# Packed attention with a gated feed-forward: the first product of six of eight batches as Strassen's seven block products

## The chip, the core and the metric

The kernel runs on one core of a Trainium2 chip. A core has four compute engines: TensorE (PE in the profile; its weight loads have a row of their own, PEld), VectorE (DVE), ScalarE (ACT) and GpSimd (POOL). SyncE (SP) issues the transfers here. Each engine takes its instructions in the order in which they are written, and engines wait for each other by semaphores. TensorE writes only to PSUM, which has eight banks of 512 float32 columns. The metric is the device time of one execution in microseconds, as a median of runs.

## The reference

Inputs: q, k, v of 8 batches x 8 heads x 576 rows x 64, p of 8 x 8 x 32 x 64, w_a and w_b of 512 x 1536, w_out of 1536 x 512.

```python
def sm_attn(qq, kk, vv):
    s = scale * np.matmul(qq, kk.transpose(0, 1, 3, 2))
    s = s - np.max(s, axis=-1, keepdims=True)
    a = np.exp(s)
    a = a / (np.sum(a, axis=-1, keepdims=True) + 1e-09)
    return np.matmul(a, vv)
p_packed = sm_attn(p, k, v)             # 32 packed rows per head
out = sm_attn(q, p_packed, p_packed)    # 576 rows attend to the 32 packed rows
...
x = out, heads side by side             # 4608 tokens x 512
a = x @ w_a
b = x @ w_b
return (a * b @ w_out)
```

## The kernel before

All of it is float32. Since `out` of a head is a2 (the second softmax, 576 x 32 per head) times the head's 32 packed rows, `x @ w_a` is a2 times a matrix G that has 256 rows (8 heads x 32) and is made for each batch from the packed rows and the weights. The **first product** of a batch is thus a2 (576 tokens x 256) times G (256 x 1536, for w_a and for w_b), the **second** is the gated h (576 x 1536) times w_out. In both, each operand is split in a high part of reduced precision (fp32r) and a rest, and high x high, high x rest and rest x high are added up in PSUM: three matmuls for each block product.

A batch runs through 12 feature tiles `ft` of 128 features. `mm1` (L378) makes one: `mm1_half` (L365) twice, for w_a and w_b, each 2 blocks of the 256 rows x 3 terms x 2 halves of the tokens = 12 matmuls of 128 x 288, so 24 per tile. ACT copies the w_a half (L385), DVE multiplies (L388), ACT takes the high part of h (L392), POOL the rest (L86 `h_lo`). `mm2_part` (L396) is the second product: 36 matmuls of 128 x 512 for a tile of 128 tokens; four or five token tiles per batch (a batch has 4.5, and odd batches do the shared one). It runs after all 12 feature tiles.

G is made by `g_tiles` (L341, matmuls at L355) from the weights in `w_ab`, which stay in SBUF, and split by ACT (L361) and DVE (L86 `glo`). These matmuls use TensorE as eight small tiles of 64 rows x 32 columns, one for each pair of a head group and a half; so do the attention products (L249 and L309 in 64 x 32, L293 in 128 x 32). The other matmuls and the transposes use the whole 128 x 128 array. Per batch `g_tiles` is called at three feature tiles (`G_AT`) and once for the next batch.

The attention of batch b+1 is cut into steps, and a table (`PLAN`) puts them between the halves of the feature tiles and between the parts of the second product of batch b; the order of each engine is as the code writes it. Batch 0 also converts the weights; it has tables of its own. PSUM: two pairs of banks (`m`) for the products, one pair (`s`) for the attention, two single banks (`x`) for G.

Of the kernel before, what the change touches and what calls it, by code (L numbers as in the profile page):

```python
# [19 lines left out]
def tile_packed_attn_gated_ffn(  # L20
# [25 lines left out]
    P = 128  # L46
# [8 lines left out]
    NT = 5  # L55
    scale = 1.0 / float(D) ** 0.5
# [3 lines left out]
    big = ep(tc.tile_pool(name="big", bufs=1))  # L60
    ld = ep(tc.tile_pool(name="ld", bufs=1))
# [8 lines left out]
    scratch = early.__enter__()  # L70

# [4 lines left out]
    w_ab = big.tile([P, NC, R, 4 * P], F32, name="w_ab")  # L76
# [154 lines left out]
    def turned(dst, src, back=0):  # L231

        tp = bank()
# [5 lines left out]
    pp = {}  # L239
# [62 lines left out]
    def stage2(b, e):  # L302

        TU = 2 * XH
        hi, lo = (t[:, e, :].rearrange("p (x u l) -> p u x l", u=2, l=TL) for t in (a2_hi, a2_lo))
        x = bank_pair(b == 1 or e == 0)
# [22 lines left out]
        a2f = work(b, f"a2f_{e}", [P, 2, XH, TL], "t2")  # L329
        nc.vector.transpose(out=a2f.rearrange("p u x l -> p (u x l)"), in_=s2.rearrange("p x j -> p (x j)"))  # L330
        nc.scalar.copy(out=hi, in_=a2f)
# [6 lines left out]
    ghi = ld.tile([P, E, 4, 2 * P], F32R, name="ghi")  # L338
    glo = ld.tile([P, E, 4, 2 * P], F32R, name="glo")
# [102 lines left out]
    def emit(b, plan, tasks={}):  # L442

        for name in plan.split():
# [45 lines left out]
    PLAN = (" |  |  | S0 | r0 | r0 |  | r0 |  | r0 Lv1 ; S1 | r1 | q0 Lk2 | r1 | r1 |  | r1 q1 Lk3 Lv2 |  |  |  | "  # L490
            "| T2 P0 |  |  | s0 s0 s1 g s0 |  | s1 | Lp4 s0 s1 s1 k2 | s0 | s0 | s1 s0 | s1 Lq2 | s1 | k3 Lq3")
# [84 lines left out]
    for b in range(B):  # L576
        plan = dict(PLAN if b else PLAN_0)
        slot, tasks, late = [0], {"g": next_g(b + 1)}, [""]

        def between():  # L580

            steps, _, late[0] = (plan.get(slot[0], "") if b + 1 < B else "").partition(";")
            emit(b + 1, steps, tasks)
            slot[0] += 1

        for ft in range(NFT):
            if b == 0 and ft % 2 and ft + 1 < NFT:
                g_tiles(b, (ft + 1, ft + 2))
            elif b and ft in G_AT:
                g_tiles(b, *G_AT[ft])  # L590
                emit(b + 1, late[0], tasks)
            mm1(b, ft, between)
        tiles = [64 + P * i for i in range(4)] if b % 2 == 0 else [P * i for i in range(5)]
        last = tiles.pop() if b == B - 1 else None
        f0 = 0
        if b == 0:
            f0 = 9
            pairs = [bank_pair() for _ in range(2)]
            banks = [pairs[i % 2][:, i // 2, :] for i in range(4)]
            for f in range(f0):  # L600
                for i, c0 in enumerate(tiles):
                    mm2_part(banks[i], c0, [f])
                between()
# [51 lines left out]
```

## Time and profile before

| | |
|---|---|
| time before, three runs | 730.17, 731.78, 732.37 us (median 731.78) |
| profiled execution: span from first to last instruction | 730.0 us (the profile shows no time around it) |
| TensorE busy | 716.7 us, 98% of the span |
| VectorE, ScalarE, GpSimd busy | 302.3, 284.6, 212.4 us (41%, 39%, 29%) |
| batches 2 to 6 | 82.2 to 82.4 us with four token tiles, 90.5 us with five |
| first and second product in the chain of waits | 40.5% and 40.6% |
| memory traffic | 58.32 MB, mean 80 GB/s |

The chain of waits is the work that ended last, followed back from the last instruction. The columns of a list of groups are: line, engine, operation, tile written <- tiles read, shape, count, then busy time in us and mean ns of one, then idle time before them. A matmul's mean contains the pipeline's depth; its pace is read from the chain, where matmuls follow each other. A float32 matmul in small tiles leaves two records, so x16 is eight instructions.

### The profile page before, as it was taken

The page shows a single profiled execution, that of the slowest core. Times are in us where ns is not written, and L with a number is a line of the kernel's source. Part 1 is how long each engine was busy: PE and PEld are TensorE (multiplying, and loading weights), DVE is VectorE, ACT ScalarE, POOL GpSimd, SP SyncE. Part 2 cuts the span into 40 slices and gives each one's busy share as a digit, 9 for nine tenths or more (in the row PEclk, how much of TensorE's full clock was granted, in tenths as well). Part 3 has the DMA queues.
Part 4 walks back from the last instruction along what each step waited for, and adds up shares of the span by engine and source line. Part 5 has one row for each costly group of instructions (what it writes and reads, how often), then busy time and mean ns, then how long its engine had stood idle before and what let it go on. Part 6 is the DMA issues. An engine that isn't in the chain of part 4 may idle for free.

```text
span 730.0 us, 14037 instructions
## 1 busy us (share of the span) xinstructions
PE 716.7 (98%) x5990; PEld 611.8 (84%) x5990; DVE 302.3 (41%) x487; ACT 284.6 (39%) x519; POOL 212.4 (29%) x154
## 2 busy tenths in 40 slices
PE   6899999999999999999999999999999999999998
PEld 4488878898888988898888988889888898898987
DVE  2888655456204562245602455044620546023100
ACT  3788743543115531454204542155311553135200
POOL 0486742334003340133202342033400334023300
PEclk9999999999999999999999999999999999999999
DMA  8999864350501505033320333215050100000011
GB/s 237 386 261 302 228 135 80 68 107 7 109 30 33 99 7 109 16 66 71 61 63 15 67 72 68 56 33 99 2 108 30 34 2 16 30 15 2 1 33 40
DMA packets 171006, 58.32 MB, mean 80 GB/s; under 512 B 140608, under 2 KB 158784, under 8 KB 170944
## 3 DMA queue, kind: packets, MB, share of 16 engines
q1 hardware_dynamic: 170944, 57.43, 32.4%
q8 instruction: 47, 0.77, 0.5%
q14 instruction: 15, 0.12, 0.1%
HBM read 47.97 MB, written 9.44 MB: 79 GB/s over the span
## 4 chain that ended last, share of the span: by engine, by line
PE 94%; DVE 2%; DMA 1%; SPq 1%; ACT 1%; issue 1%; DVEq 0%; ACTq 0%
PE m L399 41%; PE m L373 40%; PE x L355 4%; PE s L293 2%; PE m L355 1%; PE s L249 1%; PE s L283 1%; PE s L309 1%; DVE w_ab L200 1%; SPq L111 1%; DMA kn<-in_k_dram 1%; DMA nat<-in_k_dram 1%; PE x L236 0%; PE s L355 0%; PE x L147 0%
## 5 line engine op out<-in xcount | busy, mean ns | idle before, releaser
L399 PE MATMUL m<-wo,h_hi 128*128 128x512 f32 (+1 forms) x888 | 268.8, 385 | 0.0
L86 POOL TENSOR_TENSOR h_lo<-asb,h_hi 128x576 fp32r<-128x576 f32 x96 | 138.5, 1443 | 399.4 <-ACT h_hi L392 397.0
L388 DVE TENSOR_TENSOR asb<-m,asb 128x576 f32<-128x576 f32 x96 | 72.7, 757 | 306.8 <-PE m L373 296.1
L399 PEld LDWEIGHTS m<-wo,h_hi 128*128 128x128 f32 x888 | 164.2, 188 | 35.9 <-issue 3.4
L373 PE MATMUL m<-a_hi,ghi 128*128 128x288 f32 x768 | 169.0, 301 | 1.6 <-ACT ghi L361 1.5
L399 PE MATMUL m<-wo,h_lo 128*128 128x512 f32 (+1 forms) x444 | 170.3, 384 | 0.0
L373 PE MATMUL m<-a_lo,ghi 128*128 128x288 f32 x768 | 164.4, 296 | 0.3 <-DVE a_lo L86 0.3
L373 PEld LDWEIGHTS m<-a_hi,ghi 128*128 128x128 f32 x768 | 123.0, 189 | 23.0 <-issue 7.8
L373 PE MATMUL m<-a_hi,glo 128*128 128x288 f32 x768 | 133.6, 296 | 0.0
L373 PEld LDWEIGHTS m<-a_lo,ghi 128*128 128x128 f32 x768 | 123.3, 188 | 0.5 <-DVE a_lo L86 0.5
L392 ACT CAST h_hi<-asb 128x576 fp32r<-128x576 f32 x96 | 64.6, 673 | 140.4 <-DVE asb L388 140.3
L373 PEld LDWEIGHTS m<-a_hi,glo 128*128 128x128 f32 x768 | 112.9, 188 | 0.2 <-DVE glo L86 0.2
L399 PEld LDWEIGHTS m<-wo,h_lo 128*128 128x128 f32 x444 | 83.4, 188 | 16.7
L385 ACT COPY asb<-m 128x576 f32<-128x576 f32 x96 | 61.6, 641 | 31.1 <-PE m L373 24.3
L434 ACT COPY asb<-m 128x512 f32<-128x512 f32 x24 | 14.1, 586 | 133.4 <-PE m L399 132.3
L86 DVE TENSOR_TENSOR glo<-x,ghi 128x512 fp32r<-128x512 f32 x68 | 43.5, 681 | 4.4 <-ACT ghi L361 3.9
L119 DVE STREAM_TRANSPOSE xT<-nat 128x1152 f32<-128x1152 f32 x28 | 38.3, 1368 | 1.4 <-DMA nat<-in_k_dram 1.4
L361 ACT CAST ghi<-x 128x512 fp32r<-128x512 f32 x68 | 36.5, 591 | 5.2 <-PE x L355 5.2
L355 PE MATMUL x<-w_ab,ppT 64*32 64x512 f32 x544 | 37.8, 591 | 0.3 <-DVE w_ab L200 0.3
L434 ACT COPY wo_f<-m 128x512 f32<-128x512 f32 x11 | 6.4, 586 | 53.8 <-PE m L399 53.8
L189 ACT ACTIVATE raw<-raw 128x512 f32<-128x512 f32 x36 | 23.1, 686 | 1.7 <-DMA raw<-in_moe_w_a_dram 1.6
L327 POOL TENSOR_TENSOR t<-t,sum 128x576 f32<-128x576 f32 x14 | 16.5, 1178 | 24.9 <-DVE sum L326 24.9
(117 smaller groups left out, 474.0 us busy)
## 6 DMA issues: line engine op xcount, KB each, us to landing
nat<-in_k_dram SPq DMA_DIRECT2D x56, 144.0 KB
nat<-in_q_dram SPq DMA_DIRECT2D x56, 144.0 KB
vt<-in_v_dram SPq DMA_DIRECT2D x28, 256.0 KB
raw<-in_moe_w_a_dram SPq DMA_DIRECT2D x12, 512.0 KB
raw<-in_moe_w_b_dram SPq DMA_DIRECT2D x12, 512.0 KB
raw<-in_moe_w_out_dram SPq DMA_DIRECT2D x12, 512.0 KB
out_dram<-asb SPq DMA_DIRECT2D x17, 256.0 KB
out_dram<-wo_f SPq DMA_DIRECT2D x10, 256.0 KB
```

The costliest lines, as they stand in the source:

```text
L86: return eng.tensor_tensor(out=dst, in0=src, in1=hi.bitcast(F32), op=ALU.subtract)
L119: nc.vector.transpose(out=xT.rearrange("p h t -> p (h t)"), in_=t.rearrange("p h x d -> p (h x d)"))
L189: nc.scalar.activation(out=high, in_=high, func=AF.Prelu, scale=2.0 ** -112, alpha=-2.0 ** 32)
L327: eng.tensor_tensor(out=s2, in0=s2, in1=sum2.unsqueeze(2).broadcast_to([P, TU, J]), op=ALU.mult)
L355: nc.tensor.matmul(out=gps[e][J * r:J * r + J, 0:2 * P * n], lhsT=ppT[rows, 2 * (b % 2), r, :], rhs=w if n == 2 else w[:, fts[0] % 2], sta ...
L361: nc.scalar.copy(out=hi, in_=part)
L373: nc.tensor.matmul(out=ps[:, half, 0:HS], lhsT=gt[:, kt, ft % 4, cols], rhs=at[:, kt, HS * half:HS * half + HS], start=(n == 0 and kt == 0 ...
L385: nc.scalar.copy(out=asb, in_=pa[:, :, 0:HS])
L388: nc.vector.tensor_tensor(out=asb, in0=pb[:, :, 0:HS], in1=asb, op=ALU.mult)
L392: nc.scalar.copy(out=hh, in_=flat)
L399: nc.tensor.matmul(out=o[:, cols], lhsT=ht[:, c0:c0 + P], rhs=wt[:, cols], start=(ft == 0 and n == 0), stop=(ft == NFT - 1 and n == 2))
L434: nc.scalar.copy(out=ob, in_=o)
```

## The change

Batches 0 and 1 stay as they were in their first product, the second product of batch 1 and all of batches 2 to 7 are rewritten as a sequence of **periods**, one per feature tile (`period`). Rows of a2 in two blocks, the features of w_a and w_b, and the two halves of the tokens make a 2 x 2 by 2 x 2 block product; it is done with seven products instead of eight (in a form that shares sums). Their left operands are seven combinations of the blocks of G, their right operands seven combinations of the blocks of a2.

- Each product is three matmuls of 128 x 288 (`product`), 21 per feature tile. PSUM pair X and pair V are held throughout; results are added up in them across products, with copies taken between them (`d`, `c2`).
- `make_g` makes G of one feature tile per period, two periods ahead; `sum_g` forms the six other combinations (ACT 2, DVE 3, POOL 1 instructions), `split_g` splits them (ACT 128 x 768, POOL 128 x 768).
- The weights no longer stay in SBUF: in batch 1 `keep_weights` writes them to DRAM in twelve pieces of 512 KB, and `load_kept` reads one back per period, two buffers.
- The second product is done in two K halves of six feature tiles; its matmuls (12 or 15 per period) stand between the products (`fill`). After the first half ACT copies the sum to SBUF (`keep_part`), after the second DVE adds the two (`put_out`).
- `half_sums` (POOL, four subtractions) and `half_parts` (ACT and DVE) prepare the combinations of a2 for the next batch. Attention steps stand at three places of each period (`STEPS`).

```diff
+    def half_sums(b):
+        x0, x1, tf = a2f_of[b, 0], a2f_of[b, 1], late["tf"]
+        sub = lambda out, a, c: nc.gpsimd.tensor_tensor(out=out, in0=a, in1=c, op=ALU.subtract)
+        sub(tf[:, 1], x1[:, 1], x0[:, 1])
+        sub(x0[:, 1], x0[:, 1], x0[:, 0])
+        sub(tf[:, 0], x1[:, 1], x0[:, 1])
+        sub(tf[:, 2], x1[:, 0], tf[:, 0])
...
+    PRODUCTS = {1: (0, a_t[0, 0]), 2: (1, a_t[1, 0]), 3: (3, a_t[1, 1]), 4: (2, x_t[2]),
+                5: (5, a_t[0, 1]), 6: (6, x_t[0]), 7: (4, x_t[1])}
...
+    def product(n, k, bank, first):
+        j, (hi, lo) = PRODUCTS[k]
+        gh, gl = G_hi[:, n % 3, j], G_lo[:, n % 3, j]
+        for i, (g, t) in enumerate(((gh, hi), (gh, lo), (gl, hi))):
+            nc.tensor.matmul(
+                out=bank[:, n % 2, 0:HS], lhsT=g, rhs=t, start=(first and i == 0), stop=(i == 2), skip_group_check=True)
...
+    def make_g(n):
+        b = NB + n // NFT
+        w = wr_of.pop(n)
+        x = bank_pair(True)
+        for r in range(R):
+            for e in range(E):
+                rows = slice(64 * e, 64 * e + 64)
+                nc.tensor.matmul(
+                    out=x[J * r:J * r + J, e, 0:2 * P], lhsT=ppT[rows, 2 * (b % 2), r, :], rhs=w[rows, r, :],
+                    start=True, stop=True)
+        load_kept(n + 2)
+        return x
...
+    def split_g(n):
+        nc.scalar.copy(out=G_hi[:, n % 3, 1:7], in_=gs)
+        lo_part(G_lo[:, n % 3, 1:7], gs, G_hi[:, n % 3, 1:7], nc.gpsimd)
...
+    def period(n, fills, steps):
...
+        x = make_g(n + 2) if more else None
+        if more:
+            sum_g(n + 2, x)
+        split_h(n - 1)
+        if here:
+            product(n, 5, X, False)
+        if there:
+            product(n + 1, 1, X, True)
+            product(n + 1, 2, V, True)
+        if here or there:
+            d = d_of[n] = lp.tile([P, 2, HS], F32, name="d", bufs=2)
+            nc.scalar.copy(out=d[:, both], in_=X[:, both, 0:HS])
+        fill(fills[0])
+        if here or there:
+            nc.vector.tensor_tensor(out=d[:, both], in0=V[:, both, 0:HS], in1=d[:, both], op=ALU.add)
+        flush()
+        emit_steps(b + 1, steps[0])
+        if here:
+            product(n, 3, X, False)
+        if there:
+            product(n + 1, 6, X, False)
+            c2 = c2_of[n + 1] = lp.tile([P, HS], F32, name="c2", bufs=2)
+            nc.scalar.copy(out=c2, in_=X[:, k1, 0:HS])
+        if more:
+            split_g(n + 2)
+        if here:
+            hf = hf_of[n] = sm.tile([P, 2, HS], F32, name="asb")
+            nc.vector.tensor_tensor(out=hf[:, 1], in0=X[:, k0, 0:HS], in1=d[:, k0], op=ALU.mult)
+        fill(fills[1])
+        flush()
+        emit_steps(b + 1, steps[1])
+        if here:
+            product(n, 4, V, False)
+        if there:
+            product(n + 1, 7, V, True)
+        if here:
+            c2 = c2_of.pop(n)
+            nc.vector.tensor_tensor(out=c2, in0=V[:, k0, 0:HS], in1=c2, op=ALU.add)
+            nc.gpsimd.tensor_tensor(out=hf[:, 0], in0=d_of.pop(n - 1)[:, k0], in1=c2, op=ALU.mult)
+        fill(fills[2])
+        flush()
+        emit_steps(b + 1, steps[2])
...
+    STEPS = {0: ("S0 r0", "", "Lq1"), 1: ("S1 r1", "r0", ""), 2: ("r0", "r1", ""), 3: ("r0", "", "q0 Lv1"),
+             4: ("r1", "", "q1 Lk2"), 5: ("r1", "P0", "Lv2 Lk3"), 6: ("s0 s0", "T2", "Lp4 s0"), 7: ("s1 s1", "s0", "s1"),
+             8: ("s0", "s1", "s0"), 9: ("s1", "", "s1 t"), 10: ("", "u0", "u1 k2"), 11: ("", "u2", "u3 k3 Lq2")}
...
+        period(n, (6, 4, 5) if half_b % 2 else (5, 3, 4), STEPS[ft])
```

In `STEPS`, S0 and S1 are the scores of the first softmax, r0 and r1 its further steps, s0 and s1 the steps of the second, P0 and T2 transposes, k, q the turning of loaded inputs, L loads, t `half_sums`, u0 to u3 `half_parts`.

On TensorE, before: the end of a feature tile in batch 1 and the start of the next. L249 is the scores of the next batch, L355 G for three feature tiles.

```order
L373 MATMUL m<-a_hi,glo 128x288 x4
L249 MATMUL s<-xT_2190,pT 32x288 x2
L249 MATMUL s<-xT_2279,pT 32x288 x2
L249 MATMUL s<-xT_2190,pT 32x288 x2
L249 MATMUL s<-xT_2279,pT 32x288 x2
L355 MATMUL m<-w_ab,ppT 32x256 x8
L355 MATMUL x<-w_ab,ppT 32x512 x8
L373 MATMUL m<-a_hi,ghi 128x288 x2
```

The small-tile matmuls stand together here, between whole-array matmuls. Now, on TensorE, the start of period 1 of batch 4 (L722 is the second product, L772 `make_g`, L759 the products 5, 1 and 2):

```order
L722 MATMUL x_4422<-wo_1406,h_hi10_512 128x512 x2
L722 MATMUL x_4422<-wo_1406,h_lo10_513 128x512
L772 MATMUL s_4481<-wr_4321,ppT_100 32x256 x8
L759 MATMUL m_2228<-a2_hi_97,G_hi_2173 128x288
L759 MATMUL m_2228<-a2_lo_98,G_hi_2173 128x288
L759 MATMUL m_2228<-a2_hi_97,G_lo_2174 128x288
L759 MATMUL m_2228<-a2_hi_97,G_hi_2173 128x288
```

and, a little later in the same period, the scores (L255) on their own:

```order
L722 MATMUL x_4514<-wo_1262,h_hi6_504 128x512 x2
L722 MATMUL x_4514<-wo_1262,h_lo6_505 128x512
L255 MATMUL s_4523<-xT0_4310,pT_99 32x288 x2
L255 MATMUL s_4523<-xT1_4384,pT_99 32x288 x2
L255 MATMUL s_4523<-xT0_4310,pT_99 32x288 x2
L255 MATMUL s_4523<-xT1_4384,pT_99 32x288 x2
L759 MATMUL m_2228<-a2_hi_97,G_hi_2173 128x288
```

G and the scores are now two stretches of small tiles with whole-array work between them. Over the whole program TensorE goes into small tiles 43 times before and 124 times now.

On POOL, the end of period 8 and period 9 of batch 2 (L332 is a step of the second softmax, L92 with 768 columns `split_g`, L848 half of the gating, L785 `sum_g`, L602 `half_sums`):

```order
L332 TENSOR_TENSOR t1_2963<-t1_2963,sum2_3119 128x576
L92 TENSOR_TENSOR G_lo_2174<-gs_2175,G_hi_2173 128x768
L848 TENSOR_TENSOR asb_3134<-d_3031,c2_3058 128x288
L785 TENSOR_TENSOR gs_2175<-gs_2175 128x256
L92 TENSOR_TENSOR h_lo8_509<-asb_3134,h_hi8_508 128x2x9x32
L332 TENSOR_TENSOR t1_3048<-t1_3048,sum2_3192 128x576
L92 TENSOR_TENSOR G_lo_2174<-gs_2175,G_hi_2173 128x768
L848 TENSOR_TENSOR asb_3207<-d_3111,c2_3130 128x288
L602 TENSOR_TENSOR tf_2176<-t1_3224,t2_3152 128x288
L602 TENSOR_TENSOR t2_3152<-t2_3152 128x288
```

Two more L602 rows follow, and then the L785 row of period 10. Before, POOL had one `h_lo` row per feature tile and four rows of the second softmax per batch.

On ACT, the end of period 11 of batch 2 and the start of period 0 of batch 3 (L821 copies `d`, L832 `c2`, L790 is `split_g`, L616 `half_parts`, L728 `keep_part`, L780 and L781 `sum_g`, L800 the high part of h, L271 the exponential of the first softmax):

```order
L821 COPY d_3331<-m_2228 128x576
L832 COPY c2_3345<-m_2228 128x288
L790 CAST G_hi_2173<-gs_2175 128x768
L616 CAST a2_hi_97<-t2_3152 128x288
L616 CAST a2_hi_97<-t1_3224 128x288
L616 CAST tx_hi_2177<-tf_2176 128x288
L728 COPY part_2179<-x_3279 128x512
L780 COPY gs_2175<-s_3380 128x256
L781 CAST G_hi_2173<-s_3380 128x128
L800 CAST h_hi11_514<-asb_3349 128x2x9x32
L821 COPY d_3408<-m_2228 128x576
L271 ACTIVATE t1_3429,rs_3430<-s_3417,nmx_3426 128x512
```

Before, ACT had two instructions per feature tile (L385, L392), twelve of L361 per batch, and the same attention steps.

226 lines of the change are left out of this document (186 added, 40 removed).

## The prediction

> **What bounds the kernel now.** I read the page's busy line and its chain of waits first, then the busy time by batch, then the chain in the last batch piece by piece.
>
> ```profile
> span 730.0 us, 14037 instructions
> PE 716.7 (98%) x5990; PEld 611.8 (84%) x5990; DVE 302.3 (41%) x487; ACT 284.6 (39%) x519; POOL 212.4 (29%) x154
> PE 94%; DVE 2%; DMA 1%; SPq 1%; ACT 1%; issue 1%; DVEq 0%; ACTq 0%
> ```
>
> TensorE is busy for 98% of the span and carries 94% of the chain. By batch (stretch, its length, then busy us and instructions of each engine):
>
> ```profile
> core 0: us, PE busy (x) PEld busy (x) DVE busy (x) ACT busy (x) POOL busy (x), PEclk, DMA share, GB/s
> 296.64:387.17 90.53, 90.53 (x757) 78.37 (x756) 34.39 (x55) 30.91 (x57) 21.72 (x16) 1.00 0.27 56
> 642.20:726.80 84.60, 84.58 (x600) 75.33 (x599) 14.76 (x21) 23.47 (x39) 17.12 (x12) 1.00 0.06 18
> ```
>
> From batch 2 on TensorE never pauses, at the full clock, and the other engines work for 24 to 38% of a batch. So a matmul taken out shortens the span, as long as TensorE stays fed; and what TensorE loses between matmuls must be looked for inside its busy time. The chain shows it (start us, us, what):
>
> ```profile
> 601.90 0.22 PE x L236 x2
> 602.12 4.78 PE m L373 x36
> ...
> 608.89 0.43 PE s L355 x16
> 609.32 32.88 PE m L399 x144
> 642.20 6.38 PE m L373 x48
> 648.58 0.59 PE m L355 x16
> 649.17 0.86 PE x L355 x16
> 650.03 9.78 PE m L373 x72
> ```
>
> First-product matmuls (128 x 288) run at 6.38/48 = 0.1329 us, second-product ones at 32.88/144 = 0.2283. The eight G matmuls of 256 columns take 0.43 us when they follow other small tiles (608.89), but 0.59 behind whole-array work (648.58): **0.16 for going into small tiles**. Behind them 72 products take 9.78 where 72 x 0.1329 = 9.57: **0.21 for coming out**. Together 0.37 us for each stretch of small tiles. The transposes at 601.90, which use the whole array, cost nothing of the kind: the 36 products behind them take 36 x 0.1329 = 4.78.
>
> **The change part by part.**
>
> *Products.* Batches 2 to 7 have 72 feature tiles; 24 matmuls each become 21. 72 x 3 = 216 fewer x 0.1329 = **-28.7 us**. That the three matmuls of a product now write the same half bank one after the other costs nothing: L399 does so at its pace of 0.2283.
>
> *G.* Before, three tiles of G cost 8 x 256 and 8 x 512 columns, now 24 x 256: the same columns, and by 0.43 and 0.86 above the same time. **0.** The second product keeps its columns too; its last token tile is cut in halves over 18 instead of 36 matmuls each, 0.2 us less, which I drop.
>
> *Stretches of small tiles.* G now comes in every period instead of in four places per batch joined with the attention, and the attention stands alone. The order shows 124 such stretches for 43: 81 more x 0.37 = **+30.0 us**. Bounds: if going in costs nothing (0.16 could be a wait of the sequencer rather than of the array) 81 x 0.21 = 17.0; 81 x 0.38 = 30.8 at the top. I take 0.37, since `make_g` has just the shape of the row at 648.58, with a 128 x 512 matmul ahead instead of a 128 x 288 one.
>
> The Trainium skill, "TensorEngine Tiling (Array Packing)", Key Properties, says that changing the tiling mode (not just the tile) drains TensorE, without a price. "TensorE: Matmul & The Clock Gate", Single matmul latency, gives a matmul that hides no drain about 166 ns beyond its columns; two per stretch would be 81 x 2 x 0.166 = 26.9 us as an estimate from that page, against 30.0 by the rows. The trace agrees on the mechanism: 0.16 and 0.21 around small tiles, none around whole-array transposes.
>
> So TensorE's own work comes out even: -28.7 + 30.0 = +1.3. What remains is whether it stays fed. The rows for that (groups: busy us, mean ns of one, idle before):
>
> ```profile
> L86 POOL TENSOR_TENSOR h_lo<-asb,h_hi 128x576 fp32r<-128x576 f32 x96 | 138.5, 1443 | 399.4 <-ACT h_hi L392 397.0
> L388 DVE TENSOR_TENSOR asb<-m,asb 128x576 f32<-128x576 f32 x96 | 72.7, 757 | 306.8 <-PE m L373 296.1
> L392 ACT CAST h_hi<-asb 128x576 fp32r<-128x576 f32 x96 | 64.6, 673 | 140.4 <-DVE asb L388 140.3
> L385 ACT COPY asb<-m 128x576 f32<-128x576 f32 x96 | 61.6, 641 | 31.1 <-PE m L373 24.3
> L119 DVE STREAM_TRANSPOSE xT<-nat 128x1152 f32<-128x1152 f32 x28 | 38.3, 1368 | 1.4 <-DMA nat<-in_k_dram 1.4
> L327 POOL TENSOR_TENSOR t<-t,sum 128x576 f32<-128x576 f32 x14 | 16.5, 1178 | 24.9 <-DVE sum L326 24.9
> ```
> ```profile
> L86 POOL TENSOR_TENSOR wo<-wo_f,wo 128x512 fp32r<-128x512 f32 x12 | 15.5, 1294 | 10.3 <-ACT wo L225 9.9 <-POOL h_lo L86 0.3
> L255 DVE TENSOR_REDUCE nmx<-s 128x1 f32<-128x576 f32 x15 | 11.2, 747 | 1.4 <-PE s L249 1.4
> L286 ACT COPY t<-s 64x128 f32<-64x128 f32 x14 | 3.6, 257 | 0.0
> ```
> ```profile
> 648.67 0.76 DVE L388 TENSOR_TENSOR asb<-m,asb 128x576 f32<-128x576 f32 x1 [2.44 <-PE m L373]
> 649.46 0.67 ACT L392 CAST h_hi<-asb 128x576 fp32r<-128x576 f32 x1 [1.76 <-DVE asb L388]
> 650.27 1.43 POOL L86 TENSOR_TENSOR h_lo<-asb,h_hi 128x576 fp32r<-128x576 f32 x1 [1.77 <-ACT h_hi L392]
> ```
>
> Handing over: DVE starts 0.2 to 0.3 after TensorE's last slot, ACT 0.03 after DVE ends, POOL 0.14 after ACT ends. ACT costs 0.86 ns a column between L286 and L385, so 288 columns take 0.40, and 768 by L392 0.84. POOL costs 2.33 ns a column between 512 and 576, so the split of 768 takes 1.89. Half of a 576-column product on POOL, 288, takes 0.6 to 0.8; I take 0.7.
>
> *The period.* TensorE's part is G 0.43 + 0.37, 21 products 2.79, and 12 or 15 matmuls of the second product 2.74 or 3.42: **6.33 or 7.01 us** without attention. Against it stands a ring from product 6 to the next product 6: ACT's `c2` copy 0.26 + 0.40, ACT's split of G 0.84 (behind it in ACT's queue), POOL's split 0.14 + 1.89, POOL's half of the gating behind that 0.70, ACT's high part of h 0.10 + 0.67, the `d` copy queued behind it 0.64, then products 3 and 6, which may not write X before it: 0.10 + 0.80. Sum **6.54**. A period of 12 fills without an attention block therefore waits 0.2; one of 15, none. There are 18 such (periods 8 to 11 of batches 2, 4 and 6, and 0 to 5 of batch 7): **+4**. Without cover (POOL's 0.8, hand-overs of 0.3) 10.
>
> *Scores, periods 0 and 1.* Between `d` and `c2` ACT now has the exponential, which waits for DVE's maximum:
>
> ```profile
> 307.87 0.69 ACT L265 ACTIVATE t<-s,nmx 128x512 f32<-128x512 f32 x1 [0.41 <-DVE nmx L256]
> 308.75 0.20 ACT L265 ACTIVATION_READ_ACCUMULATOR t<-s,nmx 128x1 f32 x1
> ```
>
> From the end of the scores: 0.26 + 0.75 + 0.2 + 1.1 (307.87 to 308.95) = 2.3, where `c2` would have started after 0.8 + 0.26. The ring grows by 1.2 to 7.8, the period by 0.85 (scores 0.48 + 0.37) to 7.2 or 7.9. Two periods wait up to 0.8 each in batches 3 and 5 (12 fills), hardly in the others; with POOL's split late for product 2, **+5** in all.
>
> *Batch ends.* `half_sums` puts four POOL subtractions of 0.7 (2.8) into period 9, ahead of period 10's G. POOL's split of G starts about 1.1 late, which makes the ring 7.6 and the wait 1.3 (12 fills) or 0.6. Then `half_parts` puts five subtractions on DVE, in front of `c2`'s sum, and L119 (1.37) twice. Such a subtraction can be held by POOL:
>
> ```profile
> 355.61 1.16 POOL L327 TENSOR_TENSOR t<-t,sum 128x576 f32<-128x576 f32 x1 [2.10 <-DVE sum L326]
> 355.81 1.57 DVE L86 TENSOR_TENSOR a_lo<-t,a_hi 128x576 fp32r<-128x576 f32 x1 [0.34 <-ACT a_hi L331]
> 357.49 0.78 DVE L330 STREAM_TRANSPOSE t<-t 128x576 f32<-128x576 f32 x1
> ```
>
> It took 1.57 beside POOL, which ended at 356.77. DVE is then 1.3 late with `d`, which product 4 awaits before it may write V. 1.3 + 0.3 + 1.3 in batches 2, 4 and 6, half of it in 3 and 5: **+12**. If DVE is never held and POOL's idle time takes the four, 4; if each of the five is held for a whole split of 1.89, 20.
>
> (The Trainium skill, "SBUF — State Buffer", Who interferes with whom: a DVE instruction with two SBUF inputs and a GpSimd one that reads SBUF exclude each other. The two rows agree.)
>
> *Streaming.* Each period reads 512 KB, asked for two periods (12.7 us) ahead.
>
> ```profile
> 2.74 4.45 DMA kn<-in_k_dram
> ```
>
> That is a 512 KB load: hidden. At the start the last piece must be written and the first read, 8.9 us, against 18 matmuls (4.1) and the copying of the last weights under the first product: 0 to 5, **+2**.
>
> Sum on the profiled execution: 730.0 - 28.7 + 30.0 + 4 + 5 + 12 + 2 = 754.3. Its span is 1.8 under the median of the runs (731.78), so **756 us**, 3.3% slower.
>
> **The rivals.**
>
> *The array switches for less (faster).* If 0.16 at the entry was the sequencer waiting and the ring has slack (all stalls together 3), then 730 - 28.7 + 17.0 + 3 + 1.8 = 723. For: nothing on TensorE waits long at 648.58. Against: transposes enter free. It decides once 81 x price + stalls falls under 26.5.
>
> *Nothing waits.* The full price, but POOL and ACT keep up: 730 + 1.3 + 1.8 = 733. For: they are busy under 40% now. Against: POOL goes from 1.44 us per feature tile to 0.6 + 1.44 + 1.89 + 0.7 = 4.6 of 6.33, in a ring.
>
> *The ring sets the pace.* If each turn takes one more (POOL held by DVE, ACT behind its attention steps), 7.54: 36 periods lose 1.2 and 36 0.5 = 62, of which attention blocks on TensorE (0.6 in a mean period of five batches) cover some 30; 754 + 32 + 1.8 = 788. Against: 1443 for `h_lo` holds with DVE at work.
>
> **How the numbers follow.** Forecast 0.57, the ring 0.17, faster 0.16, nothing waits 0.10. The lower end of the range is the least of each stall with 0.30 per stretch: 730 - 28.7 + 24 + 5 + 1.8 = 732; the upper, 786, stops 2 us short of the ring. This leaves out the faster case and the ring's tail. A change of 0.3% (2.2 us) is about what can be told here: the faster rival falls below it; of the second rival I count nearly all as within. Faster 0.16, same 0.09, slower 0.75.
>
> **What would show it.** In the chain after, a lone `make_g` of eight instructions should take 0.59 and the 9 products behind it 1.2 + 0.2. If G's columns stand there with 0.43 and no gap, the third term is wrong. TensorE's idle time should lie ahead of product 3, released by ACT's `d` copy, of product 2 (POOL) and, in periods 10 and 11, of product 4 (DVE); 20 to 30 us in all. If waits for the weights' loads appear, the streaming term is wrong. Even periods of 8 and more would show the ring.

## The result and the profile after

| | before | after |
|---|---|---|
| median of the runs | 731.15 us (730.17 to 732.37) | 772.06 us (770.80 to 773.32) |
| ratio, 95% interval | | 1.0555 (1.0534 to 1.0577) |
| span of the profiled execution | 730.0 us | 771.2 us |
| TensorE busy; not busy (span less busy) | 716.7; 13.3 us | 735.8; 35.4 us |
| mean granted TensorE clock | 1.000 | 0.991 |

The changed kernel is 5.6% slower. The prediction had the direction, and 24 of the 41 us. As a number, 772 lies as far above the forecast of 756 as it lies below the 788 of the rival in which the ring sets the pace; only the periods below tell the two apart. The page of the changed kernel (span, busy line, chain of waits by engine):

```profile
span 771.2 us, 15740 instructions
PE 735.8 (95%) x6140; PEld 573.5 (74%) x6140; DVE 420.6 (55%) x832; ACT 362.8 (47%) x760; POOL 471.8 (61%) x394
PE 71%; POOL 13%; DVE 7%; ACT 5%; issue 2%; DMA 1%; SPq 0%; DVEq 0%; POOLq 0%; ACTq 0%
```

TensorE's share of the chain fell from 94% to 71%. The rest is now POOL, DVE and ACT, although each of them works for 47 to 61% of the span only: they are not full, they are late in particular places. To find these, take the length of a period, from one `make_g` (L772) to the next. The timeline of TensorE in batch 7, which has no attention beside it, first with 12 fills per period, then with 15:

```profile
676.60 0.66 PE L772 MATMUL s<-wr,ppT 64*32 64x256 f32 x16
682.95 0.66 PE L772 MATMUL s<-wr,ppT 64*32 64x256 f32 x16
...
708.32 0.66 PE L772 MATMUL s<-wr,ppT 64*32 64x256 f32 x16
715.35 0.66 PE L772 MATMUL s<-wr,ppT 64*32 64x256 f32 x16
```

6.35 and 7.03 us, where the prediction had worked out 6.33 and 7.01 for TensorE alone. The chain at the start of batch 2 shows the parts (start, us, what):

```profile
204.56 0.59 PE s L772 x16
205.16 1.38 PE m L759 x9
```

A lone `make_g` takes 0.59, and the nine products behind it 1.38 where 9 x 0.1329 = 1.20: the two prices of a stretch, 0.16 and 0.18, where the prediction had 0.16 and 0.21. So where nothing else is going on, TensorE's own work is what was said, +1.3 us in all. The loss lies in the periods that are not quiet. Their lengths, worked out from the starts of `make_g` in each timeline (12 fills: periods 6 to 11 of batches 2, 4, 6, and 0 to 5 of batches 3, 5, 7; 15 fills in the others):

| | period 9, 10 (12 fills) | period 11, batches 2 to 6 | period 0, batches 3 to 6 | first `make_g` to period 0 of batch 2 |
|---|---|---|---|---|
| after | 7.24, 7.08 | 9.17 to 10.43 | 8.92 to 8.98 | 25.9 |
| least in any run with small-tile matmuls for G in every period | 6.33, 6.34 | 6.34 (12 fills), 7.02 (15) | 7.15 (12), 7.84 (15) | 19.9 |

The last row is put together from the experiments below. Summed over all twelve positions, the five batches 2 to 6 take some 30 us more than these least lengths: 16 in period 11, 6 in period 0, 5 in periods 9 and 10, 3 in the others. Batch 7 adds 0.8, and the start 7 (a wait of 0.8 for the first weights among it). With +1.3 that is some 39 of the 41.2 us between the two profiled spans; the other 2 I can't place, and a wait that all these runs share is hidden in the least lengths.

**The batch end.** The timeline of POOL, then of DVE, then of TensorE at the end of batch 2 (period 10 begins at 280.17, period 11 at 287.25; in brackets the idle time ahead and what ended it):

```profile
282.50 0.81 POOL L602 TENSOR_TENSOR tf<-t,t 128x288 f32<-128x288 f32 x1
...
285.16 0.81 POOL L602 TENSOR_TENSOR tf<-t,tf 128x288 f32<-128x288 f32 x1
285.93 0.73 POOL L785 TENSOR_TENSOR gs<-gs 128x256 f32<-128x256 f32 x1
286.62 1.43 POOL L92 TENSOR_TENSOR h_lo<-asb,h_hi 128x576 fp32r<-128x576 f32 x1
288.01 1.82 POOL L92 TENSOR_TENSOR G_lo<-gs,G_hi 128x768 fp32r<-128x768 f32 x1
290.96 1.25 POOL L848 TENSOR_TENSOR asb<-d,c 128x288 f32<-128x288 f32 x1 [1.13 <-DVE c L847]
```
```profile
288.38 2.14 DVE L92 TENSOR_TENSOR a_lo<-t,a_hi 128x288 fp32r<-128x288 f32 x2 [2.54 <-ACT a_hi L616]
290.44 0.45 DVE L847 TENSOR_TENSOR c<-m,c 128x288 f32<-128x288 f32 x1
290.81 0.74 DVE L92 TENSOR_TENSOR tx_lo<-tf,tx_hi 128x576 fp32r<-128x576 f32 x1
291.47 1.36 DVE L125 STREAM_TRANSPOSE xT<-nat 128x1152 f32<-128x1152 f32 x1
...
296.76 1.88 DVE L92 TENSOR_TENSOR a_lo<-t,a_hi 128x288 fp32r<-128x288 f32 x1 [0.60 <-ACT a_hi L616]
...
298.92 0.44 DVE L92 TENSOR_TENSOR a_lo<-t,a_hi 128x288 fp32r<-128x288 f32 x1
```
```profile
288.40 0.40 PE L759 MATMUL m<-a_hi,G_hi 128*128 128x288 f32 x1
290.20 0.40 PE L759 MATMUL m<-a_lo,G_hi 128*128 128x288 f32 x1 [1.41 <-DVE a_lo L92]
```

The four subtractions (3.4 us with their gaps) delay POOL's sum of G and so its split (288.01, in period 11 although it is period 10's). DVE's rests of a2 are released at 288.38, run into that split and take 2.14 for two; one of the same shape takes 0.44 later (298.92), and 1.88 beside POOL's next split (296.76). They end just after the split does (289.83), and TensorE stands for 1.41: its first product with the new a2 (product 1) reads the rest that DVE is late with. Then the clock falls (windows: stretch, length, busy us of each engine, PEclk, DMA share, GB/s):

```profile
291.00:292.00 1.00, 0.97 (x5) 0.91 (x6) 1.00 (x2) 0.00 (x0) 1.00 (x1) 0.79 0.00 0
292.00:293.00 1.00, 1.00 (x4) 0.81 (x3) 1.00 (x2) 0.76 (x2) 0.21 (x1) 0.50 0.00 0
...
295.00:296.00 1.00, 1.00 (x7) 0.84 (x6) 0.31 (x1) 0.74 (x2) 0.60 (x1) 1.00 1.27 199
```

Some 3.4 us at half the clock: 1.7 us lost after the wait had ended. Of the five batch ends only those of batches 2 and 6 show this fall. TensorE counts as busy at half the clock too, which is one reason why its busy time grew by 19 us and not by 1.

**The start.** TensorE's timeline in the first period (batch 1's second product), with the wait for the first weights ahead of it:

```profile
178.61 0.67 PE L772 MATMUL s<-wr,ppT 64*32 64x256 f32 x16 [0.84 <-DMA wr<-w_kept]
...
183.24 0.39 PE L722 MATMUL x<-wo,h_lo 128*128 128x512 f32 x1
186.86 1.22 PE L722 MATMUL x<-wo,h_hi 128*128 128x512 f32 x2 [3.24 <-ACT part L728]
```

ACT's copy of a finished sum (`keep_part`) stands behind the casts of `half_parts`, which wait for POOL's subtractions; then the next 5.29 us run at a granted 0.50.

### The profile page after: what moved, and what is told of

Read it like the earlier page. It is cut to its first block, busy times and chain, and to the rows that moved or that the text cites. A ratio compares the mean times of both kernels' runs of the same rounds, so it can differ in the third digit from the quotient of the medians.

```text
span 771.2 us, 15740 instructions
## 1 busy us (share of the span) xinstructions
PE 735.8 (95%) x6140; PEld 573.5 (74%) x6140; DVE 420.6 (55%) x832; ACT 362.8 (47%) x760; POOL 471.8 (61%) x394
## 4 chain that ended last, share of the span: by engine, by line
PE 71%; POOL 13%; DVE 7%; ACT 5%; issue 2%; DMA 1%; SPq 0%; DVEq 0%; POOLq 0%; ACTq 0%
PE x L722 25%; PE m L759 20%; PE m L384 9%; POOL G_lo L92 5%; PE m L410 4%; PE s L772 4%; POOL h_lo L92 2%; POOL t L332 2%; PE s L299 1%; POOL tf L602 1%; POOL asb L848 1%; PE s L314 1%; PE s L255 1%; DVE xT L125 1%; PE x L366 1%
## 5 line engine op out<-in xcount | busy, mean ns | idle before, releaser
L722 PE MATMUL x<-wo,h_hi 128*128 128x512 f32 (+1 forms) x780 | 249.4, 394 | 3.2 <-ACT part L728 3.2
L92 POOL TENSOR_TENSOR G_lo<-gs,G_hi 128x768 fp32r<-128x768 f32 x72 | 132.7, 1843 | 93.8 <-ACT G_hi L790 93.8
L92 POOL TENSOR_TENSOR h_lo<-asb,h_hi 128x576 fp32r<-128x576 f32 x96 | 138.7, 1445 | 50.7 <-ACT h_hi L403 46.9
L722 PEld LDWEIGHTS x<-wo,h_hi 128*128 128x128 f32 x780 | 141.5, 191 | 22.7 <-ACT part L728 3.7
L722 PE MATMUL x<-wo,h_lo 128*128 128x512 f32 (+1 forms) x390 | 153.0, 392 | 0.0
L759 PE MATMUL m<-a_hi,G_hi 128*128 128x288 f32 x288 | 98.6, 342 | 8.0 <-ACT d L821 4.5
L759 PEld LDWEIGHTS m<-a_hi,G_hi 128*128 128x128 f32 x288 | 54.2, 188 | 55.3 <-issue 35.8
L785 POOL TENSOR_TENSOR gs<-gs 128x256 f32<-128x256 f32 x72 | 53.0, 736 | 67.9 <-DVE gs L783 48.5
L780 ACT COPY gs<-s 128x256 f32<-128x256 f32 x72 | 26.8, 372 | 134.8 <-POOL G_lo L92 71.2
L759 PE MATMUL m<-a_lo,G_hi 128*128 128x288 f32 x288 | 85.8, 298 | 4.5 <-DVE a_lo L92 4.2
L759 PE MATMUL m<-a_hi,G_lo 128*128 128x288 f32 x288 | 86.0, 299 | 0.5 <-POOL G_lo L92 0.3
L722 PEld LDWEIGHTS x<-wo,h_lo 128*128 128x128 f32 x390 | 74.2, 190 | 12.0
L832 ACT COPY c<-m 128x288 f32<-128x288 f32 x72 | 28.7, 399 | 92.2 <-PE m L759 91.6
L848 POOL TENSOR_TENSOR asb<-d,c 128x288 f32<-128x288 f32 x72 | 61.0, 847 | 12.8 <-DVE c L847 12.8
L759 PE MATMUL m<-tx_hi,G_hi 128*128 128x288 f32 x216 | 64.8, 300 | 0.0
L790 ACT CAST G_hi<-gs 128x768 fp32r<-128x768 f32 x72 | 60.5, 841 | 7.7 <-POOL gs L785 7.7
L759 PE MATMUL m<-tx_hi,G_lo 128*128 128x288 f32 x216 | 63.9, 296 | 0.0
L759 PE MATMUL m<-tx_lo,G_hi 128*128 128x288 f32 x216 | 63.8, 295 | 0.0
L800 ACT CAST h_hi<-asb 128x576 fp32r<-128x576 f32 x72 | 48.8, 678 | 26.5 <-POOL asb L848 26.3
```

Source lines behind the costliest of these rows:

```text
L92: return eng.tensor_tensor(out=dst, in0=src, in1=hi.bitcast(F32), op=ALU.subtract)
L722: nc.tensor.matmul(out=o[:, cols], lhsT=ht[:, c0:c0 + P], rhs=wt[:, cols], start=(ft == fts[0] and n == 0), stop=(ft == fts[-1] and n == 2))
L759: nc.tensor.matmul(out=bank[:, n % 2, 0:HS], lhsT=g, rhs=t, start=(first and i == 0), stop=(i == 2), skip_group_check=True)
L785: nc.gpsimd.tensor_tensor(out=gs[:, 2:4], in0=gs[:, 0:2], in1=gs[:, 5:6].broadcast_to([P, 2, P]), op=ALU.subtract)
L790: nc.scalar.copy(out=G_hi[:, n % 3, 1:7], in_=gs)
L800: nc.scalar.copy(out=view(h_hi[ft]), in_=src)
```

## The experiments

All medians are of four runs, each with the ratio to the kernel before in its 95% interval; "the changed kernel" is 1.0555. "Less" is worked out from the two ratios, one hundredth being 7.3 us.

### The stretches of small tiles: G by whole-array work

```diff
-        for r in range(R):
+        for r in range(2):
             for e in range(E):
-                rows = slice(64 * e, 64 * e + 64)
-                nc.tensor.matmul(
-                    out=x[J * r:J * r + J, e, 0:2 * P], lhsT=ppT[rows, 2 * (b % 2), r, :], rhs=w[rows, r, :],
-                    start=True, stop=True)
+                nc.tensor.transpose(x[:, e, P * r:P * r + P], w[:, 2 * e + r, 0:P], ident)
```

> The eight small-tile matmuls of make_g are replaced by four whole-array transposes of the same length on TensorE (0.43 us); G then holds other values, everything behind it runs as before. If a stretch of small tiles costs 0.37 us for changing the array over, the 72 lone ones go: 771 - 72 x 0.37 = 744 to 746, and the undisturbed periods fall from 6.34 and 7.02 to 5.97 and 6.65. If instead the ring over ACT and POOL holds the periods (worked out at 6.54), they stay near 6.3 with 12 fills, and the time falls by 0 to 12 at most: 759 to 771. Anything between says that a second limit stands between 5.97 and 6.34.

761.67 us, 1.0414 (1.0398 to 1.0431): 10 less instead of 27, in the second range. The periods say why. TensorE's timeline in batch 7 with 12 fills and a weight load that waits for ACT's copy of `d`, then the chain with 15 fills:

```profile
691.38 0.60 PE L771 MATMUL s<-ident,wr 128*128 128x128 f32 x4
...
694.28 0.19 PEld L759 LDWEIGHTS m<-a_hi,G_hi 128*128 128x128 f32 x1 [0.38 <-ACT d L818]
...
697.59 0.60 PE L771 MATMUL s<-ident,wr 128*128 128x128 f32 x4
```
```profile
711.11 0.44 PE s L771 x4
711.54 1.20 PE m L759 x9
...
717.79 0.44 PE s L771 x4
```

With 15 fills a period falls from 7.03 to 6.68, by 0.35: the price of a stretch. The four transposes take 0.44 and the nine products behind them 1.20, so that nothing is paid at either end. With 12 fills it stops at 6.21 instead of 5.97, and TensorE waits for ACT's copy of `d`. That is the ring of the prediction, 6.2 and not 6.54; it lies 0.13 under the quiet period and becomes the limit as soon as TensorE gets faster. At the batch ends, where other engines are late anyway, the gain vanishes: period 11 in batch 3 is 10.33 against 9.17.

### The start

```diff
-    for i in range(4):
-        half_parts(NB, i)
...
-        period(n, (12, 12, 12) if n == -2 else (10, 8, 9), ("", "", ""))
+        period(n, (12, 12, 12) if n == -2 else (10, 8, 9), ("u0", "u1", "u2 u3") if n == -2 else ("", "", ""))
```

> half_parts for batch 2 is moved from ahead of the first period into its steps, so that the copies of keep_part don't stand on ACT behind casts that wait for POOL. If TensorE's 3.2 us of waiting and the half-speed matmuls behind it (about 2.9 us lost) come from that queue: 771 - 6 = 765. If POOL's half_sums, which end at 185, hold the first period anyway, only the place of the wait changes: 769 to 772.

766.64, 1.0481 (1.0466 to 1.0497): 5.4 less. The two periods ahead of batch 2 take 19.9 instead of 25.9, and the first of them runs at the full clock (0.78 in the changed kernel). The queue on ACT was the cause of the wait of 3.24, which is gone.

### The batch ends: without half_sums and half_parts

```diff
+            elif b > NB and name[0] in "tu":
+                continue
             elif name == "t":
                 half_sums(b)
```

> half_sums and half_parts are left out for batches 3 to 7, which use the combinations of a2 of batch 2; nothing else is taken out. By the lengths of the periods the batch ends lose about 25 us (periods 9 to 11 and the next period 0), by the prediction's sum 12. If that work is the cause: 771 - 25 = 746 (750 if the turning of k still holds DVE), or 759 by the predicted size. If the batch ends are slow for another reason (the turning of inputs, the exponential, loads): 765 to 771.

749.00, 1.0243 (1.0222 to 1.0264): 22.8 less, by the first expectation. Period 11 of batch 2, on TensorE, from its `make_g` (here L774) to the next:

```profile
286.08 0.66 PE L774 MATMUL s<-wr,ppT 64*32 64x256 f32 x16
292.43 0.66 PE L774 MATMUL s<-wr,ppT 64*32 64x256 f32 x16
```

Period 11 is 6.34 or 7.02 in all batches, which gives back 16 us, and period 0 is 7.17 or 7.84 (6.35 in batch 7), which gives back 6.6. Periods 9 and 10 keep their 7.22 and 7.06: these are not the batch end's.

### The turnings of k

```diff
-             4: ("r1", "", "q1 Lk2"), 5: ("r1", "P0", "Lv2 Lk3"), 6: ("s0 s0", "T2", "Lp4 s0"), 7: ("s1 s1", "s0", "s1"),
-             8: ("s0", "s1", "s0"), 9: ("s1", "", "s1 t"), 10: ("", "u0", "u1 k2"), 11: ("", "u2", "u3 k3 Lq2")}
+             4: ("r1", "", "q1 Lk2"), 5: ("r1", "P0", "Lv2 Lk3"), 6: ("s0 s0", "T2", "Lp4 s0"), 7: ("s1 s1", "s0", "s1 k2"),
+             8: ("s0", "s1", "s0 k3"), 9: ("s1", "", "s1 t"), 10: ("", "u0", "u1"), 11: ("", "u2", "u3 Lq2")}
```

> The last two turnings of k (DVE, 1.4 us each) are moved from periods 10 and 11 to 7 and 8. If DVE's backlog at the batch end is theirs, six batch ends give back 1 to 2 us each: 760 to 765. If the hold is that of DVE by POOL in half_parts alone, the time stays within 769 to 772; if the turnings now hold the second softmax in periods 7 and 8, it rises by up to 6.

769.72, 1.0515 (1.0492 to 1.0537): 2.9 less, which is barely clear of the noise, since the two intervals touch; it lies in the second range. The periods show the effect more plainly: period 0 of batches 3 to 6 falls from 8.9 to 7.6 to 7.8, 4.8 us in all. So it was DVE's turning of 1.37 us at the end of period 11 that held period 0, where the prediction had put the exponential. In the changed kernel the scores of period 0 wait 1.0 to 1.3 us, in batch 3 so:

```profile
302.49 0.72 PE L255 MATMUL s<-xT,pT 64*32 64x288 f32 x16 [1.32 <-DVE G_lo L92]
```

The scores write the pair of PSUM banks (`s`) from which DVE must first have read G, and DVE's reading of G stands behind the turning. Period 11 stays long (9.2 to 10.5) and is longer than before in batch 4.

### G in pairs

```diff
+        if more and n % 2 == 0:
+            x = bank_pair(True)
+            make_g(n + 2, x)
+            make_g(n + 3, x)
+            sum_g(n + 2, x)
...
+        if x is not None:
+            sum_g(n + 3, x)
```

Two buffers for the sums of G, one instead of two for the outputs, and the small-tile steps of even periods one place later; the turnings of k as in the run above.

> G of two feature tiles is made in one stretch of small tiles every second period (the attention steps of those periods and two turnings of k move to other places). 36 stretches fewer. By the price of a stretch alone: 771 - 36 x 0.37 = 758, and 3 less for the turnings: 755. If the ring over ACT and POOL, which showed at 6.20 us in a period without the changeover, sets a floor: a period without G needs 5.54 of TensorE with 12 fills and takes 6.2, one with both G 6.77, so a pair takes 12.97 against 12.68 now; with 15 fills 7.45 + 6.25 = 13.7 against 14.04. Then 18 such pairs lose 0.3 and 18 gain 0.3, and only the turnings are left: 766 to 770.

768.73, 1.0499 (1.0475 to 1.0523). A quiet pair with 12 fills takes 12.99 (12.97 expected by the floor, 12.68 as two single periods, 12.31 by TensorE alone), with 15 fills 13.71. The second expectation holds: the ring eats the 36 stretches saved.

### The subtractions on DVE

```diff
-        sub = lambda out, a, c: nc.gpsimd.tensor_tensor(out=out, in0=a, in1=c, op=ALU.subtract)
+        sub = lambda out, a, c: nc.vector.tensor_tensor(out=out, in0=a, in1=c, op=ALU.subtract)
```

> The four subtractions of half_sums are moved from POOL (0.81 each) to DVE. If POOL's 3.3 us in period 9 make its split of G late, and everything at the batch end follows from that, five batch ends give back 2 to 3.5 us each: 754 to 761. If the price is what DVE does there (half_parts' rests, held by POOL's split, and the turnings), which stays: 768 to 774, and DVE's 1.8 us more in period 9 may show there.

763.63, 1.0440 (1.0416 to 1.0464): 8.4 less, a little short of the first range. Not all of it lies at the batch ends: the start takes 22.4 instead of 25.9, as `half_parts` there waits for the same subtractions. Period 11 falls to 8.1 to 8.3, 7.9 us in all, period 10 of the even batches rises by 0.2, and period 0 stays at 8.95 to 8.98. At the end of batch 2 TensorE waits 0.20 for DVE's rest, where it waited 1.41, and the mean granted clock is 1.000, so that the two falls of the clock, some 3.4 us, are part of the 7.9. So POOL's subtractions are about a third of what the run without the two helpers gave back at the batch ends.

### The split of G on DVE

```diff
         nc.scalar.copy(out=G_hi[:, n % 3, 1:7], in_=gs)
-        lo_part(G_lo[:, n % 3, 1:7], gs, G_hi[:, n % 3, 1:7], nc.gpsimd)
+
+    def split_g_lo(n):
+
+        lo_part(G_lo[:, n % 3, 1:7], gs, G_hi[:, n % 3, 1:7], nc.vector)
...
             nc.gpsimd.tensor_tensor(out=hf[:, 0], in0=d_of.pop(n - 1)[:, k0], in1=c2, op=ALU.mult)
+        if more:
+            split_g_lo(n + 2)
```

> The split of G's six combinations (128 x 768) is moved from POOL (1.84 us, 72 times) to DVE, behind the sum for c2 in DVE's queue. The ring then has no POOL split ahead of the gating. If POOL's split is what the waits hang on: periods 9 and 10 with 12 fills fall from 7.23 and 7.06 to 6.35 (5 us in all), the batch ends give back about half of their 20: 755 to 758; periods that wait for nothing stay at 6.34 and 7.02. If DVE, which goes from 421 to about 495 us, is now the late one, or is held by POOL's rests of h as often as before: 768 to 780.

754.21, 1.0302 (1.0276 to 1.0328): 18 less, the most of any single edit that leaves nothing out, and just past the first range. Periods 9 and 10 fall to 6.34 exactly, period 11 to 7.6 to 8.8. The two groups concerned, in this run and, behind it, the gating in the changed kernel:

```profile
L851 POOL TENSOR_TENSOR asb<-d,c 128x288 f32<-128x288 f32 x72 | 102.9, 1429 | 152.0 <-DVE c L850 151.7
L92 DVE TENSOR_TENSOR G_lo<-gs,G_hi 128x768 fp32r<-128x768 f32 x72 | 68.3, 949 | 4.6 <-ACT G_hi L790 4.6
```
```profile
L848 POOL TENSOR_TENSOR asb<-d,c 128x288 f32<-128x288 f32 x72 | 61.0, 847 | 12.8 <-DVE c L847 12.8
```

DVE needs 0.95 for what took POOL 1.84. But POOL's gating now starts just behind DVE's split (653.26 and 653.10 in batch 7), and it takes 1.43 instead of 0.85: POOL is held by DVE this time.

### Three edits together

The start, G in pairs and the split on DVE.

> Three edits together: half_parts of batch 2 in the steps of the first period, G in pairs, the split of G on DVE. If they add up, with no ring left under the pairs: 771 - 5.5 - 13 - 14 - 3 = 735. If the floor under a period stays at 6.2 whoever splits G, the pairs bring nothing: 771 - 5.5 - 14 - 3 = 748. Under 729 it would beat the kernel before.

742.21, 1.0145 (1.0124 to 1.0166), between the two expectations. A quiet pair with 12 fills takes 12.64, with 15 fills 13.71 (13.67 by TensorE alone). The floor has moved, but not away.

### The gating on DVE too, paired and single

Against the three edits together (parts of the changed lines):

```diff
-            nc.gpsimd.tensor_tensor(out=hf[:, 0], in0=d_of.pop(n - 1)[:, k0], in1=c2, op=ALU.mult)
+            nc.vector.tensor_tensor(out=hf[:, 0], in0=d_of.pop(n - 1)[:, k0], in1=c2, op=ALU.mult)
...
-9: ("s1", "", "s1 t"), 10: ("", "u0", "u1")
+9: ("s1", "", "s1 t0"), 10: ("t1", "u0", "u1")
...
-                if 2 <= slot[0] and slot[0] % 2 == 0 and kept[0] < NFT:
+                if 2 <= slot[0] and kept[0] < NFT:
```

> The three edits of the version with pairs (half_parts in the first period's steps, G in pairs, split of G on DVE), and three more: the second half of the gating also on DVE (POOL's took 1.44 us beside DVE's split, against 0.85 before), half_sums in two pieces, two subtractions before and two behind period 10's work on POOL, and the weights written out one piece per step instead of one per two steps of batch 1. If the ring over POOL is what holds a pair at 12.64 us with 12 fills instead of 12.31, and periods 8 to 11 of the batches, 742 goes down by 1 (batch 7), 3 (periods 8 and 9), 6 (10 and 11) and 3.5 (start): 727 to 729, just under the kernel before. If DVE, now the busiest after TensorE (about 68%), is late in its place: 736 to 745.

> The same as the run with the gating on DVE, but G made singly, one stretch of small tiles per period, as in the changed kernel, with the two turnings of k in periods 7 and 8. With no ring under it, single against paired is the price of 36 stretches and nothing else: 36 x 0.35 to 0.37 = 12.6 to 13.3 us more than the paired run (some 741). If a floor under the periods remains, or the two sets of attention places weigh in, the two differ by less than 8.

Paired 750.61, 1.0264 (1.0247 to 1.0281), single 751.15, 1.0276 (1.0260 to 1.0291). Both first expectations fall, and 750.61 lies above the second range too (736 to 745); the two runs differ by 0.5, as the second one of the pair had it. The paired run is 8 us slower than the run before. It has two other edits beside the gating on DVE, but the last version below has these as well, leaves the gating on POOL and takes 741.84, so that the gating is the likely cause. The pairs gain nothing. A quiet pair takes 12.54, hardly less than two single periods; periods 6 and 7 of batches 2 and 4 together go from 14.51 to 15.77, of 3 and 5 from 15.66 to 16.9. DVE is at 67% of the span and, with the softmax beside it, late where TensorE needs it: TensorE waits for DVE's rests of G 13 times, 11.4 us in all. This run was to show the price of a stretch with no ring under it; it doesn't, since another limit took the ring's place.

### Only the order on ACT

```diff
         x = make_g(n + 2) if more else None
         if more:
             sum_g(n + 2, x)
-        split_h(n - 1)
...
             nc.scalar.copy(out=d[:, both], in_=X[:, both, 0:HS])
+        split_h(n - 1)
         fill(fills[0])
```

> One edit in the changed kernel: the high part of h on ACT (and its rest on POOL) is written behind the copy of d instead of ahead of it, so that the copy, which product 3 awaits, no longer stands behind POOL's gating; all else as it was. If that queueing on ACT closes the ring: periods 9 and 10 of batches 2, 4 and 6 fall from 7.23 and 7.06 to 6.34 (5 us in all), and the batch ends give back part of their 20, some 5: 760 to 766; quiet periods stay at 6.34 and 7.02. If POOL's lateness reaches TensorE in another way (G's rest for product 2, or the combinations of a2), 768 to 773.

768.84, 1.0513 (1.0497 to 1.0529): 3.1 less, at the foot of the second range. Period 9 falls from 7.23 to 6.66, period 10 only from 7.07 to 6.95, period 2 of even batches from 7.9 to 7.57; period 11 of these is 10.84, longer than before. In the changed kernel, period 9 read so on POOL and ACT:

```profile
271.76 1.16 POOL L332 TENSOR_TENSOR t<-t,sum 128x576 f32<-128x576 f32 x1 [0.41 <-PE m L759]
272.88 1.83 POOL L92 TENSOR_TENSOR G_lo<-gs,G_hi 128x768 fp32r<-128x768 f32 x1
274.68 0.81 POOL L848 TENSOR_TENSOR asb<-d,c 128x288 f32<-128x288 f32 x1
```
```profile
274.75 0.37 ACT L780 COPY gs<-s 128x256 f32<-128x256 f32 x1 [2.40 <-POOL G_lo L92]
275.01 0.27 ACT L781 CAST G_hi<-s 128x128 fp32r<-128x128 f32 x1
275.51 0.67 ACT L800 CAST h_hi<-asb 128x576 fp32r<-128x576 f32 x1 [0.23 <-POOL asb L848]
276.09 0.63 ACT L821 COPY d<-m 128x576 f32<-128x576 f32 x1
```

The second softmax's 1.16 on POOL goes ahead of the split, the split ahead of the gating, and ACT's copy of `d` stands behind both the cast of h (for the gating) and the copy into `gs`, which may not start before POOL has read the old sums there. The edit takes away one of these two links; the second, `gs` with a single buffer, I had not seen in the code. That it is what remains in period 10 is argued from these rows, not tried alone.

### All that helped

The three edits together, with the cast of h behind the second sum of G, two of the four subtractions behind POOL's sums, the weights written out early; the gating on POOL.

> The three edits that gave 742 (half_parts in the first period's steps, G in pairs, split of G on DVE), the gating back on POOL, and: the high part of h behind the copy of d, two of the four subtractions of half_sums behind both of POOL's sums of G, the weights written out one piece per step. If ACT's queue closes the ring: pairs with 12 fills go from 12.64 to 12.31 (1 us in batch 7), periods 8 and 9 give 3, 10 and 11 give 4 to 8, the start 1.7: 728 to 733, level with the kernel before. If DVE's split, which holds the gating on POOL, or DVE's rests at the batch end are the floor: 738 to 744.

741.84, 1.0147 (1.0130 to 1.0164), in the second range and no better than 742.21. The quiet pairs, though, have reached TensorE's floor. The timeline in batch 7, 12 fills:

```profile
664.08 1.09 PE L773 MATMUL s<-wr,ppT 64*32 64x256 f32 x32
676.40 1.09 PE L773 MATMUL s<-wr,ppT 64*32 64x256 f32 x32
```

12.32 against 12.31, and 12.68 for two single periods: a stretch less is worth 0.36, here too. What is left lies beside the attention: periods 8 and 9 of the even batches take 13.39 (12.31 by TensorE), 10 and 11 take 14.5 to 16.1, of batches 3 and 5 15.03 (13.67). That is about 16 us over the program, so that this layout, if none of it remained, would come to some 726 by these rows: an estimate, and no version of mine reached it. None of the kernels is as fast as the one before.

## Why the prediction was right, and where it wasn't

**Products -28.7, G 0, stretches +30.0: right.** The quiet periods come out at 6.34 and 7.02 against 6.33 and 7.01. The price of 0.37 per stretch, taken from two rows of before, is measured three times, for the stretches of G: 0.59 for the lone `make_g` and 0.18 behind it, 0.35 less per period without the changeover, 0.36 per stretch saved in pairs. No run takes out a stretch of the attention alone. The rival in which the array switches for less is out.

**The ring, +4: the step failed, though the ring exists.** It turns at 6.2, not 6.54, and costs the quiet periods nothing. Its time is lost where I had not put any: periods 9 and 10 with 12 fills (+0.9 and +0.7, 4.8 us in three batches), since POOL has a softmax step ahead of the split of G there. Both are gone when the split leaves POOL. That 4.8 comes near the 4 is luck: the places differ. I had added up the links as if ACT took them one by one (with G by whole-array work, the split of G starts 0.30 us after the copy of `c2`, which takes 0.40) and had not asked what else stands in POOL's queue.

**Scores, +5: mostly another cause.** Period 1 waits 0.7 and 0.3 in batches 3 and 5 (7.85 and 7.47 against 7.16) and not elsewhere, about as said. Period 0 waits in every batch, for the turning of k that DVE still has from period 11 and behind which it reads G: with that moved, 4.8 us vanish, 1.2 per batch. Some 2 us are left of the step as I had put it; whether the exponential makes them wasn't tried. Here too the size came out by luck.

**Batch ends, +12: right in its two causes, too small, and wrong in its places.** Leaving out the two helpers gives back 22.8 us, 16 of it in period 11 (period 0's wait goes with them too, so the 4.8 of the turnings are no sum beside it). As predicted, POOL's subtractions make its split late (about a third, by the run with them on DVE), and DVE's rests are held by that split: two of them took 2.14 at one place and a single one 1.88 (at 296.76). Mis-sized were three things: each subtraction 0.81 and not 0.7; each of the two lots of rests held for a whole split, which I had kept for the upper bound; and the half clock after the wait, some 1.7 us at the end shown, for which I had no term; it came at two of the five ends. The places were others: period 10, where I had put a wait of 1.3, takes 7.06 (in even batches) with the helpers and without them, and it is not product 4 that waits for `d`, but product 1 for the rest of a2 itself (1.41) and, behind batches 3 and 5, product 2 for DVE's sum into `c2` (1.19 and 1.42).

The Trainium skill, "SBUF — State Buffer", Who interferes with whom, says that a DVE instruction with two SBUF inputs contends with a GpSimd one that reads SBUF, and that the order of issue decides which of them blocks. The runs agree in both directions: DVE takes 2.14 for two behind POOL's split, POOL 1.43 instead of 0.85 behind DVE's.

**Start and streaming, +2: 7.** The streaming is hidden as said, but for 0.84 at the very start. The 5.4 that one edit gave back are ACT's queue (3.2) and the clock after it. I had looked at the weights' way through DRAM and not at what `half_parts`, just ahead of the first period, puts into ACT's queue ahead of `keep_part`.

**Idle time.** 22 us more on TensorE (35.4 against 13.3), within the 20 to 30 named. ACT's copy of `d` ends 4.5 us of it, as named; POOL's split for product 2 hardly shows (0.3). DVE ends the most, but ahead of the scores (5.0) and of products 1 and 2 (7.7), not of product 4; ACT's `keep_part` ends 3.2 at the start. The 24 to 38% that I read for the other engines in every batch hold for batch 2; in batch 7 it is 17 to 28%, and nothing in the sum hangs on it. The rival in which the ring sets every period is out, and so is the one in which nothing waits.

## What to carry to other kernels

A saving in matmuls is not a saving in instructions for the other engines: 216 matmuls less (28.7 us) here came with 81 more stretches of small tiles (30 us) and with sums and splits for POOL, DVE and ACT, and the waits for these (some 38 us, with the slow clock behind them) cost more than the matmuls gave. Before a ring is timed, write down for every link what else stands ahead of it in its engine's queue at the worst period, not at the mean one, and which single buffer it must wait to overwrite. And when a floor is taken away, expect the next one close below: 6.34, 6.2 and 5.97 (the last worked out, not reached) lay within 6% here, and the edits that took TensorE's work away gave 10 of 27 us (G by whole-array work) and 4 of 16 (pairs, with the turnings of k moved).

## What the runs showed that I had not expected

**A pause of 1.4 us can halve TensorE's clock, or not.** The last version stops at the end of batches 2 and 4 with the same two pauses, 1.37 and 0.27 us. TensorE's timeline at the one and the other:

```profile
281.66 0.37 PE L761 MATMUL m<-a_hi,G_hi 128*128 128x288 f32 x1 [1.37 <-DVE c L863]
282.44 0.41 PE L761 MATMUL m<-a_hi,G_lo 128*128 128x288 f32 x1 [0.27 <-DVE G_lo L92]
```
```profile
457.00 0.37 PE L761 MATMUL m<-a_hi,G_hi 128*128 128x288 f32 x1 [1.37 <-DVE c L863]
457.77 0.41 PE L761 MATMUL m<-a_hi,G_lo 128*128 128x288 f32 x1 [0.27 <-DVE G_lo L92]
```

and the granted clock (the number ahead of the last two) behind them:

```profile
283.00:285.00 2.00, 2.00 (x13) 1.67 (x12) 1.41 (x2) 1.34 (x3) 0.62 (x2) 1.00 0.00 0
...
460.00:462.00 2.00, 2.00 (x8) 1.81 (x8) 0.35 (x1) 0.78 (x2) 1.17 (x1) 0.50 0.00 0
```

Periods 10 and 11 take 14.55 in batch 2 and 16.07 in batch 4: the fall costs 1.5 us, in the same program at the same place. The changed kernel has it too: its batches 2, 4 and 6 end with pauses of 1.40 or 1.41 and 0.30 us, and the clock falls behind the first and the last of them only. The Trainium skill, "TensorE: Matmul & The Clock Gate", Part 1: The HAM clock gate, puts the fall behind an idle window of about 3.4 us that runs freely. The length of the fall at the batch end of the changed kernel, some 3.4 us at 0.50, agrees, and the free running would explain the two outcomes; that whole windows have to be idle doesn't agree, since pauses of 1.4 us with matmuls between them were enough. How much of a window must be idle, no run here shows.
